# One sum in place of two: the attention values of a head group added up over all four key blocks at once, and a new order for every engine

## The chip, the core and the metric

The kernel runs on one core of a Trainium2 chip. The metric is the time of one execution in microseconds (us) of device time. The core has five engines that work side by side: TensorE (PE in the profile, with its weight loads as PEld), VectorE (DVE), ScalarE (ACT), GpSimd (POOL) and SyncE (SP), which starts the DMA transfers. Each takes its own instructions strictly in the order in which they stand in its queue, and waits with a semaphore where it needs another engine's result.

## The reference, cut to what matters

```
h   = x + attention(layernorm(x))           # x is 2048 x 512, 32 heads of 16
out = h + ffn(layernorm(h))                 # ffn: (gelu(g) * u) @ w_down, width 1376

attention, for each of 4 segments of 512 rows, one after the other:
    logits = (q @ k^T) / 4 + mask           # mask hides later keys
    a_dot  = softmax(logits) @ v
    a_mem  = (phi(q) @ M) / (phi(q) @ z + 1e-6)
    o      = g * a_mem + (1 - g) * a_dot    # g = sigmoid(beta), per head
    M, z  += phi(k)^T @ v, sum of phi(k)
then o @ wo
```

## The kernel before, in words

The program is written as a list of small operations (some 4,800), each bound to one engine. A table of numbers, `ORDER`, says in which order they are issued; from it follow each engine's queue and which buffer each operation gets, because a buffer is handed out at the first operation that uses it. [...]

The attention work is cut into 16 units, each a chunk of eight heads in one segment, and each unit into two head groups of four heads; there are 32 head groups, numbered Q0 to Q31 here. For one head group the steps are:

- `project` and `vproj` (L932, L981) make q, k and v on TensorE; DMA spreads q and k into tiles `stq` and `stk`.
- `pass_a` (L1186) computes the logits once to find each row's maximum. VectorE reads the maximum out of the PSUM bank (L1196, tiles `nm`), a small transpose (L1217) turns it, and a DMA writes it back into `stq`.
- `pass_b` computes the logits again, now transposed and with the maximum taken off: five `bank` blocks (L1244). Of the four key blocks of 128 keys, numbered 0 to 3, block 0 takes two of these, blocks 1 and 3 share two, and block 2 is the last. Each fills two PSUM banks; ScalarE takes the exponential into a `row` tile (L1250), GpSimd clears the part above the diagonal (L1258).
- `accum` (L1272) multiplies the exponentials with the values and adds up over the key blocks in one PSUM bank. It runs with four tiles of 32 columns each side by side. Before the change it is two operations: key blocks 0, 1 and 3 (12 matmuls) as soon as those four banks are done, and key block 2 (4 matmuls) after the last bank.
- ScalarE copies the sum out (L1291), and DMAs, VectorE and GpSimd normalise it. `mem` (L1134, L1154) adds the memory part, `mask`/`mup` (L1097) updates the memory.

TensorE is used in three modes: whole (128 rows by 128 columns: the feed forward network, L1531 and L1596), two halves of 64 rows (L932, L981, L1154, L1186, L1217, L1244, L1352), and four strips of 32 columns (L1097, L1134, L1272). All eight PSUM banks come out of one pool, and so do the 35 `row` tiles that hold the exponentials.

After the attention come the output projection (L1345, L1352), the second layer norm and the feed forward network in two halves of 1024 rows each. Some of it is interleaved with the last head groups.

Of the kernel before, what the change touches and what calls it, by code (L numbers as in the profile page):

```python
# [56 lines left out]
    76, 0, 5, 9, 6, 1, 10, 12, 4, 7, 13, 14, 8, 16, 27, 11, 91, 18, 92, 88, 93, 15, 17, 89, 19, 77, 28, 94, 29,  # L57
    167, 30, 25, 90, 21, 23, 20, 31, 102, 821, 33, 97, 46, 822, 47, 103, 104, 32, 95, 22, 34, 825, 44, 87, 35,
    36, 24, 168, 105, 37, 42, 106, 164, 107, 110, 826, 38, 108, 827, 40, 96, 26, 82, 111, 100, 43, 828, 84, 98,
    39, 41, 109, 118, 128, 45, 81, 824, 48, 51, 50, 829, 119, 165, 830, 831, 112, 130, 99, 113, 823, 129, 114,  # L60
    115, 1608, 116, 117, 133, 134, 78, 120, 140, 121, 122, 49, 138, 169, 166, 52, 832, 124, 53, 123, 139, 144,
    127, 833, 834, 2, 835, 54, 135, 85, 55, 75, 131, 3, 132, 145, 1026, 146, 136, 137, 147, 150, 149, 148, 170,
    56, 181, 58, 253, 172, 634, 1024, 186, 254, 255, 151, 171, 256, 59, 57, 176, 1028, 184, 185, 188, 126, 182,
    190, 125, 187, 101, 141, 142, 189, 152, 257, 154, 74, 162, 143, 183, 153, 177, 179, 60, 836, 258, 178, 173,
    61, 180, 1029, 175, 67, 68, 1025, 174, 837, 62, 63, 191, 625, 192, 259, 631, 65, 64, 69, 260, 79, 70, 66,
    193, 194, 195, 197, 71, 72, 198, 632, 261, 73, 213, 214, 262, 161, 270, 196, 263, 838, 272, 199, 273, 438,
    2986, 628, 158, 264, 268, 839, 439, 267, 239, 240, 241, 242, 440, 215, 243, 274, 269, 271, 229, 230, 232,
    276, 441, 840, 86, 275, 233, 442, 217, 216, 203, 224, 227, 225, 228, 226, 277, 266, 443, 231, 279, 234, 265,
    83, 237, 204, 235, 238, 205, 206, 236, 444, 1030, 841, 278, 200, 202, 445, 157, 1031, 207, 245, 842, 446,
    248, 449, 208, 246, 201, 843, 209, 450, 212, 448, 211, 633, 210, 244, 249, 247, 635, 218, 155, 250, 280,  # L70
    447, 1032, 219, 220, 221, 844, 222, 163, 845, 156, 846, 251, 847, 292, 848, 1033, 849, 295, 406, 286, 1034,
    407, 281, 296, 287, 852, 1035, 223, 282, 293, 297, 288, 408, 299, 318, 850, 300, 298, 301, 409, 410, 283,
    319, 80, 289, 321, 294, 328, 291, 329, 290, 302, 1027, 411, 304, 636, 303, 306, 313, 159, 331, 305, 307,
    412, 316, 314, 361, 362, 363, 364, 365, 323, 308, 324, 326, 626, 332, 317, 413, 320, 353, 354, 355, 366,
    367, 368, 369, 370, 414, 327, 797, 322, 818, 1036, 315, 427, 428, 1417, 309, 310, 330, 815, 311, 312, 798,
    415, 432, 325, 434, 627, 356, 357, 358, 359, 360, 433, 252, 417, 418, 799, 416, 334, 335, 421, 422, 800,
    419, 801, 337, 333, 338, 336, 284, 339, 429, 430, 431, 420, 629, 630, 387, 1037, 285, 340, 390, 391, 350,
    351, 352, 371, 372, 388, 802, 377, 160, 380, 378, 379, 803, 392, 435, 398, 393, 395, 425, 804, 401, 436,
    396, 373, 375, 341, 374, 376, 437, 805, 399, 809, 482, 483, 484, 485, 486, 426, 808, 586, 342, 424, 806,
    389, 477, 478, 479, 480, 481, 394, 423, 587, 1038, 807, 382, 383, 384, 343, 1411, 381, 402, 2122, 466, 467,  # L80
    468, 588, 514, 385, 386, 515, 516, 517, 589, 344, 819, 1039, 345, 346, 503, 506, 504, 469, 470, 471, 397,
    493, 590, 472, 473, 474, 475, 476, 603, 607, 400, 591, 494, 496, 498, 592, 508, 820, 499, 501, 495, 511,
    505, 593, 541, 542, 497, 487, 347, 509, 543, 594, 816, 488, 781, 500, 544, 545, 518, 536, 512, 540, 608,
    510, 2113, 538, 489, 490, 507, 491, 492, 595, 1040, 609, 403, 502, 457, 539, 537, 614, 615, 596, 513, 519,
    1224, 613, 610, 458, 611, 404, 1041, 533, 1225, 612, 597, 520, 598, 1042, 817, 578, 600, 581, 602, 601, 534,
    521, 405, 535, 599, 1226, 567, 530, 579, 570, 568, 1227, 562, 571, 606, 563, 565, 546, 531, 1228, 532, 547,
    616, 1229, 548, 572, 580, 564, 573, 618, 604, 575, 348, 550, 649, 549, 582, 551, 552, 651, 617, 1230, 557,
    650, 560, 558, 1043, 767, 662, 664, 768, 553, 665, 555, 663, 554, 1231, 1420, 666, 522, 646, 648, 1418, 605,
    1232, 576, 657, 647, 661, 574, 660, 769, 652, 556, 659, 1233, 770, 1235, 656, 459, 1234, 658, 771, 566,
    1236, 654, 673, 851, 1414, 1044, 561, 1045, 569, 653, 674, 559, 577, 676, 583, 584, 683, 655, 772, 460, 524,  # L90
    525, 688, 773, 684, 678, 675, 677, 774, 686, 1046, 689, 1047, 667, 691, 685, 668, 681, 669, 1048, 679, 1049,
    1050, 1051, 1052, 727, 671, 690, 728, 729, 731, 670, 349, 775, 730, 776, 692, 694, 777, 461, 680, 717, 672,
# [1606 lines left out]
```

## Time and profile before

| | us |
|---|---|
| median of 3 runs | 746.51 |
| lowest and highest | 746.02 and 747.25 |
| the profiled execution | 746.94 |
| its span, first to last instruction | 745.2 |
| TensorE busy in the span | 729.3 (98%) |
| VectorE, ScalarE, GpSimd busy | 568.5, 511.5, 474.5 |

The profiled execution's time is 1.7 us longer than its span, and 0.43 us above the median of the runs. The attention fills the span up to about 391 us, the feed forward network the rest. TensorE's matmuls are pipelined, so one begins before the one ahead of it has ended: the time that a group of matmuls takes is read from its start to the start of what stands behind it, not from its duration.

### The profile page before, as it was taken

How to read it: one execution, taken by the hardware profiler on the slowest of the kernel's cores; microseconds unless marked ns; L12 is line 12 of the kernel's file. 1: busy time of each engine (PE TensorE's matmuls, PEld its weight loads, DVE VectorE, ACT ScalarE, POOL GpSimd, SP SyncE). 2: the span in 40 equal slices, each digit the busy share in tenths (PEclk: the TensorE clock that was granted, in tenths of full speed). 3: DMA queues.
4: the chain of work that ended last, by engine and by line, in shares of the span. 5: the costliest groups of instructions: out<-in, count | busy, mean ns of one | idle time of the engine just before them, and what ended most of it. 6: DMA issues, size and time to landing. Idle time of an engine off the chain costs nothing.

```text
span 745.2 us, 18708 instructions
## 1 busy us (share of the span) xinstructions
PE 729.3 (98%) x6496; PEld 582.5 (78%) x6496; DVE 568.5 (76%) x1812; ACT 511.5 (69%) x1078; POOL 474.5 (64%) x750
## 2 busy tenths in 40 slices
PE   7999999999999999999999999999999999999998
PEld 6887867777877777876768788888887878888886
DVE  6897879988887898899987547775688756565466
ACT  6898888797767878878676557755586453553641
POOL 5455425564536546876884887868797578659930
PEclk9999999999999999999999999999999999999999
DMA  7756647656657757776756685554334260000003
GB/s 268 203 142 163 173 127 190 177 131 189 175 155 206 211 155 200 185 219 197 194 186 219 215 258 158 108 134 103 106 106 129 67 210 19 0 1 1 0 1 113
DMA packets 89658, 107.92 MB, mean 145 GB/s; under 512 B 31468, under 2 KB 41884, under 8 KB 89564
## 3 DMA queue, kind: packets, MB, share of 16 engines
q1 hardware_dynamic: 89260, 106.34, 50.2%
q8 instruction: 51, 0.84, 0.5%
q10 hardware_dynamic: 304, 0.39, 0.2%
q14 instruction: 43, 0.35, 0.2%
HBM read 57.03 MB, written 23.53 MB: 108 GB/s over the span
## 4 chain that ended last, share of the span: by engine, by line
PE 86%; DVE 8%; ACT 2%; issue 2%; DMA 1%; SPq 0%; DVEq 0%; ACTq 0%
PE bank L1531 28%; PE bank L1596 15%; PE bank L932 9%; PE bank L1272 8%; PE bank L1244 6%; PE bank L1186 5%; PE bank L981 5%; PE bank L1352 3%; PE bank L1345 3%; DVE bank L1196 2%; DVE aside L1196 2%; PE bank L1154 1%; DMA row<-wq 1%; DVE nm L1196 1%; PE bank L798 1%
## 5 line engine op out<-in xcount | busy, mean ns | idle before, releaser
L1250 ACT ACTIVATE row<-bank 128x512 f32<-128x512 f32 x309 | 165.5, 604 | 29.8 <-PE bank L1244 25.4
L1258 POOL TENSOR_SCALAR_AFFINE_SELECT row<-row 128x256 f32<-128x256 f32 (+1 forms) x309 | 105.9, 367 | 89.9 <-ACT row L1250 87.6
L1196 DVE CUSTOM_DVE_ANT_0 aside<-bank,amask 128x384 f32<-128x384 f32 (+2 forms) x384 | 141.7, 419 | 17.4 <-PE bank L1186 10.2
L932 PE MATMUL bank<-slot,slot 64*128 64x512 f32 x720 | 114.3, 403 | 0.0
L1531 PE MATMUL bank<-slot,slot 128*128 128x512 f32 (+1 forms) x399 | 106.1, 391 | 0.0
L1196 DVE CUSTOM_DVE_ANT_0 bank<-bank,amask 128x512 f32<-128x512 f32 x128 | 86.5, 710 | 12.0 <-PE bank L1186 10.1
L1531 PEld LDWEIGHTS bank<-slot,slot 128*128 128x128 f32 (+1 forms) x399 | 73.6, 186 | 17.5 <-issue 0.4
L1501 POOL TENSOR_TENSOR slot<-row,slot 128x512 fp32r<-128x512 f32 (+2 forms) x55 | 61.6, 1125 | 39.9 <-ACT slot L1499 37.6
L1186 PE MATMUL bank<-stk,stq 64*128 64x512 f32 (+3 forms) x512 | 82.0, 331 | 2.6 <-DMA stq<-slot 0.9
L1244 PE MATMUL bank<-stq,stk 64*128 64x384 f32 (+3 forms) x512 | 81.4, 333 | 1.7 <-DVE nm L1196 0.8
L1604 DVE TENSOR_TENSOR row<-row,bank 128x512 f32<-128x512 f32 (+1 forms) x91 | 60.4, 677 | 29.6 <-PE bank L1596 29.2
L1272 PE MATMUL bank<-row,vaug 128*32 128x512 f32 (+3 forms) x988 | 78.8, 436 | 1.2 <-DVE z L1145 0.4
L932 PEld LDWEIGHTS bank<-slot,slot 64*128 64x128 f32 x720 | 73.0, 185 | 6.2 <-DVE nm L1196 0.7
L1186 PEld LDWEIGHTS bank<-stk,stq 64*128 64x128 f32 x512 | 56.5, 185 | 14.4 <-DVE nm L1196 3.7
L1244 PEld LDWEIGHTS bank<-stq,stk 64*128 64x128 f32 x512 | 56.1, 185 | 14.6 <-DVE nm L1196 3.7
L1596 PE MATMUL bank<-slot,slot 128*128 128x512 f32 (+1 forms) x228 | 59.8, 389 | 0.0
L1272 PEld LDWEIGHTS bank<-row,vaug 128*32 128x32 f32 x988 | 30.5, 109 | 34.3 <-issue 27.3
L1531 PE MATMUL bank<-stk,slot 128*128 128x512 f32 (+1 forms) x198 | 54.7, 389 | 0.0
L981 PE MATMUL bank<-slot,slot 64*128 64x256 f32 x672 | 53.4, 284 | 0.0
L672 POOL TENSOR_TENSOR slot<-row,slot 128x512 fp32r<-128x512 f32 (+1 forms) x33 | 42.6, 1293 | 16.0 <-ACT slot L667 15.8
L1538 ACT ACTIVATE row<-bank 128x512 f32<-128x512 f32 (+1 forms) x54 | 31.6, 594 | 28.3 <-PE bank L1531 27.3
L1196 DVE DVE_READ_ACCUMULATOR2_ANT nm<- 128x1 f32 x512 | 50.1, 98 | 0.0
(269 smaller groups left out, 1622.4 us busy)
## 6 DMA issues: line engine op xcount, KB each, us to landing
stq<-slot SPq DMA_DIRECT2D x96, 128.0 KB
stk<-slot SPq DMA_DIRECT2D x94, 128.0 KB
row<-x SPq DMA_DIRECT2D x31, 256.0 KB
pv_dram<-row SPq DMA_DIRECT2D x31, 256.0 KB
row<-r_dram SPq DMA_DIRECT2D x27, 256.0 KB
row<-h_dram SPq DMA_DIRECT2D x23, 256.0 KB
row<-wd SPq DMA_DIRECT2D x17, 256.0 KB
row<-wu SPq DMA_DIRECT2D x16, 256.0 KB
```

The lines of the kernel that those rows point to most:

```text
L932: return nc.tensor.matmul(pm[i].t, w[i].t[rows_of(r), wi, dc * P:(dc + 1) * P], XT[s][dc].t[rows_of(r), xi, :], start=(dc, wi, xi, ph) == ...
L981: return nc.tensor.matmul(pms[n].t[:, 256 * t:256 * t + 256], XT[s][dc].t[rows_of(r), xi, t0:t0 + P], whl[wi].t[rows_of(r), dc // 2, 256 * ...
L1186: nc.tensor.matmul(sa.t[:, c0:c0 + w], sq.t[own, p, i * P:(i + 1) * P], sk.t[own, p, 0:w], start=True, stop=True, tile_position=(64 * a, 0 ...
L1196: nc.vector.tensor_tensor_reduce(out=(sa.t[:, c0:c0 + w] if i > 2 else aside[:, turns[0]:turns[0] + w]), in0=sa.t[:, c0:c0 + w], in1=amask ...
L1244: nc.tensor.matmul(sc.t[:, c0:c0 + D - q0], sk.t[own, p, q0:q0 + P], sq.t[own, p, q0:D], start=True, stop=True, tile_position=(64 * a, 0), ...
L1250: act(w, prio, lambda sc=sc, e=e: nc.scalar.activation(e.t[:, :w], sc.t[:, :w], AF.Exp), [sc, vtab], [e])
L1258: nc.gpsimd.affine_select(v, v, pattern=pat + [[1, P]], compare_op=OP.is_ge, fill=0.0, base=0, channel_multiplier=-1)
L1272: nc.tensor.matmul(pv.t[32 * n:32 * n + 32, kb * P:D], va.t[:, 136 * kb + 17 * j:136 * kb + 17 * j + 32], e.t[:, lo:lo + D - kb * P], star ...
L1501: pool(0.14 + 2.13e-3 * (hi - lo), prio, lambda: nc.gpsimd.tensor_tensor(v.t[:, 1, :hi - lo], r.t[:, lo:hi], v.t[:, 0, :hi - lo].bitcast(F ...
L1531: nc.tensor.matmul(dst.t[:w], v.t[:, wi, c0 + j * w:c0 + (j + 1) * w], b[bk][j].t[:, xi, :], start=first and j == 0 and n == 0, stop=j == ...
L1596: nc.tensor.matmul(pm.t[:, cs], HH[p, f, s].t[:w, hi, t * P:(t + 1) * P], v.t[:w, wi, cs], start=f == fl[0] and n == 0, stop=f == fl[-1] a ...
L1604: dve(W_, prio, lambda a=a, pm=pm, cs=cs, to=to: nc.vector.tensor_tensor(to.t[:, cs], a.t[:, cs], pm.t[:, cs], op=OP.add), [pm, a], [to])
```

## The change

The two `accum` operations of a head group become one, with all 16 matmuls, behind the last `bank` block; the key blocks are added in the order 0, 1, 3, 2. The matmuls themselves are the same. Lines of the new kernel lie 2 lower up to there and 3 lower behind (L1272 is L1270, L1531 is L1528).

The table `ORDER` has 32 entries fewer and is a new one from the first row to the last; only its start is shown. One argument `mode` is added to a VectorE operation of the feed forward network (f = 9), which the program reads for TensorE's operations alone.

```
@@ ORDER @@
-    76, 0, 5, 9, 6, 1, 10, 12, 4, 7, 13, 14, 8, 16, 27, 11, 91, 18, 92, 88, 93, 15, 17, 89, 19, 77, 28, 94, 29,
...
@@ -1281,9 +1279,8 @@
             bank([(p, 0, 0)])
         for p in range(2):
             bank([(p, 1, 0), (p, 3, 3 * P)])
-        accum((0, 1, 3), False)
         bank([(0, 2, 0), (1, 2, 2 * P)])
-        accum((2,), True)
+        accum((0, 1, 3, 2), True)
@@ -1561,7 +1558,7 @@
             lo(1.23 if f != 9 else D, prio, lambda: eng.tensor_tensor(
-                hh.t[:w, 1], e.t[:w], hh.t[:w, 0].bitcast(F32), op=OP.subtract), [e], [hh])
+                hh.t[:w, 1], e.t[:w], hh.t[:w, 0].bitcast(F32), op=OP.subtract), [e], [hh], mode=None if f != 9 else 'L')
```

Two places of the new order follow. The first is TensorE's queue around the sum of head group Q14, in the middle of the attention. L1244 are logits of the next head groups, L1186 is `pass_a`, L1097 the memory update, L1154 the memory part, L1272 the sum. A name such as `bank5_70` is a PSUM bank; the rows of the sum name the exponentials' tile and the values' tile. Before:

```order
L1272 MATMUL bank5_70<-row16_117,vaug1_141 32x128
L1272 MATMUL bank5_70<-row33_134,vaug1_141 32x128
L1244 MATMUL bank4_69<-stq0_96,stk0_91 128x512
L1244 MATMUL bank2_67<-stq0_96,stk0_91 128x512
L1186 MATMUL bank3_68<-stk2_93,stq2_98 128x512
L1186 MATMUL bank0_65<-stk2_93,stq2_98 128x512
L1097 MATMUL bank7_72<-vaug0_140,row11_112 32x34 x16
L1272 MATMUL bank5_70<-row31_132,vaug1_141 32x256
L1272 MATMUL bank5_70<-row3_104,vaug1_141 32x256
...
L1154 MATMUL bank2_67<-row9_110,mb5_151 128x256
L1154 MATMUL bank3_68<-row9_110,mb5_151 128x256
L1186 MATMUL bank4_69<-stk2_93,stq2_98 128x384
```

And now (lines 2 lower):

```order
L1270 MATMUL bank7_72<-row16_117,vaug1_141 32x256
L1270 MATMUL bank7_72<-row7_108,vaug1_141 32x256
L1270 MATMUL bank7_72<-row16_117,vaug1_141 32x256
L1242 MATMUL bank3_68<-stq0_96,stk0_91 128x512
L1242 MATMUL bank2_67<-stq0_96,stk0_91 128x512
L1184 MATMUL bank0_65<-stk2_93,stq2_98 128x512
L1184 MATMUL bank5_70<-stk2_93,stq2_98 128x512
L1215 MATMUL bank6_71<-ident_168,mm0_155 32x64
L1215 MATMUL bank7_72<-ident_168,mm0_155 32x64
L1152 MATMUL bank2_67<-row8_109,mb5_151 128x256
L1152 MATMUL bank0_65<-row8_109,mb5_151 128x256
L1184 MATMUL bank3_68<-stk2_93,stq2_98 128x384
```

Before, the sum's last part stood behind four matmuls of other work and the memory update; now it stands with the rest, ahead of them, and the memory update has moved to the next sum. Between `pass_a` into a bank (bank3 before, bank0 now) and the memory part into the same bank there stood the memory update and four matmuls of the sum; now there stand two small transposes.

The second place is the start of TensorE's queue. L894 transposes the four rows of tiles of the first segment, L953 is the first projection. Before:

```order
L894 MATMUL bank4_69<-ident_168,row0_101 128x128
L894 MATMUL bank5_70<-ident_168,row0_101 128x128
L953 MATMUL bank6_71<-slot0_73,slot5_78 128x256 x2
L953 MATMUL bank7_72<-slot0_73,slot4_77 128x256 x2
L953 MATMUL bank6_71<-slot0_73,slot5_78 128x256
L953 MATMUL bank7_72<-slot0_73,slot4_77 128x256
L953 MATMUL bank6_71<-slot1_74,slot5_78 128x256 x2
L953 MATMUL bank7_72<-slot1_74,slot4_77 128x256 x2
L894 MATMUL bank1_66<-ident_168,row2_103 128x128
```

And now:

```order
L892 MATMUL bank4_69<-ident_168,row1_102 128x128
L892 MATMUL bank5_70<-ident_168,row1_102 128x128
L892 MATMUL bank6_71<-ident_168,row3_104 128x128
L892 MATMUL bank7_72<-ident_168,row3_104 128x128
L892 MATMUL bank1_66<-ident_168,row3_104 128x128
L892 MATMUL bank0_65<-ident_168,row3_104 128x128
L892 MATMUL bank6_71<-ident_168,row2_103 128x128
...
L951 MATMUL bank3_68<-slot0_73,slot4_77 128x256 x2
```

Rows of the third and fourth tile were transposed in the middle of the projection before; now all four come ahead of it (of the last tile's four transposes three are left out).

## Rows read from the trace of the kernel before

**Rows 1.** The page: span, busy time of each engine, its 40 slices
```profile
span 745.2 us, 18708 instructions
PE 729.3 (98%) x6496; PEld 582.5 (78%) x6496; DVE 568.5 (76%) x1812; ACT 511.5 (69%) x1078; POOL 474.5 (64%) x750
...
PE   7999999999999999999999999999999999999998
...
PEclk9999999999999999999999999999999999999999
```

**Rows 2.** Three stretches (start, attention, feed forward): busy us and instruction counts
```profile
0.00:24.00 24.00, 18.16 (x131) 16.08 (x132) 15.65 (x51) 17.37 (x45) 15.19 (x36) 1.00 0.79 255
24.00:391.00 367.00, 361.11 (x4828) 280.58 (x4826) 321.68 (x1371) 296.61 (x656) 214.10 (x478) 1.00 0.65 178
391.00:742.00 351.00, 350.01 (x1542) 285.86 (x1542) 230.95 (x392) 197.51 (x378) 245.17 (x236) 1.00 0.35 102
```

**Rows 3.** The chain that ended last, shares by engine
```profile
PE 86%; DVE 8%; ACT 2%; issue 2%; DMA 1%; SPq 0%; DVEq 0%; ACTq 0%
```

**Rows 4.** What TensorE waited for: us in total, times, longest
```profile
PE bank L869 <- DMA row<-x: 3.9, 1, 3.9
PE bank L1186 <- DMA stq<-slot: 0.9, 1, 0.9
PE bank L1244 <- DVE nm L1196: 0.8, 2, 0.5
PE bank L1531 <- DVE row L1604: 0.6, 1, 0.6
```

**Rows 5.** TensorE in order of time around an undivided sum (start, us, count)
```profile
230.78 0.40 PE L1186 MATMUL bank<-stk,stq 64*128 64x384 f32 x4
231.02 0.91 PE L932 MATMUL bank<-slot,slot 64*128 64x512 f32 x6
...
232.00 0.40 PE L1244 MATMUL bank<-stq,stk 64*128 64x384 f32 x4
232.33 2.36 PE L1272 MATMUL bank<-row,vaug 128*32 128x512 f32 x32
234.62 0.96 PE L932 MATMUL bank<-slot,slot 64*128 64x512 f32 x6
```

**Rows 6.** The same around a divided sum, head group Q9
```profile
156.49 1.93 PE L1272 MATMUL bank<-row,vaug 128*32 128x512 f32 x24
158.35 0.23 PE L1217 MATMUL bank<-ident,mm 64*32 64x64 f32 x2
158.39 0.48 PE L1244 MATMUL bank<-stq,stk 64*128 64x384 f32 x4
158.81 0.64 PE L1272 MATMUL bank<-row,vaug 128*32 128x256 f32 x8
159.37 0.95 PE L1186 MATMUL bank<-stk,stq 64*128 64x512 f32 x2
```

**Rows 7.** The same around the sum of Q14, the place shown in the order
```profile
209.40 0.50 PE L1244 MATMUL bank<-stq,stk 64*128 64x512 f32 x2
209.74 0.40 PE L1186 MATMUL bank<-stk,stq 64*128 64x512 f32 x2
210.06 0.46 PE L1097 MATMUL bank<-vaug,row 128*32 128x34 f32 x32
210.34 0.66 PE L1272 MATMUL bank<-row,vaug 128*32 128x256 f32 x8
210.93 0.70 PE L1154 MATMUL bank<-row,mb 64*128 64x256 f32 x3
```

**Rows 8.** VectorE and ScalarE at that place (start, us, idle before)
```profile
210.17 0.70 DVE L1196 CUSTOM_DVE_ANT_0 bank<-bank,amask 128x512 f32<-128x512 f32 x1 [0.90 <-PE bank L1186]
...
210.05 1.09 ACT L1250 ACTIVATE row<-bank 128x512 f32<-128x512 f32 x2 [0.41 <-PE bank L1244]
```

**Rows 9.** GpSimd's clearing by form: busy, mean ns, idle before
```profile
L1258 POOL TENSOR_SCALAR_AFFINE_SELECT row<-row 128x256 f32<-128x256 f32 x185 | 73.7, 415 | 53.9 <-ACT row L1250 52.8 <-ACT mx L1221 0.4
```

**Rows 10.** Weight loads by line: busy, mean ns, idle before and its cause
```profile
L1186 PEld LDWEIGHTS bank<-stk,stq 64*128 64x128 f32 x512 | 56.5, 185 | 14.4 <-DVE nm L1196 3.7 <-issue 1.4 <-DVE slot L841 1.1
L1244 PEld LDWEIGHTS bank<-stq,stk 64*128 64x128 f32 x512 | 56.1, 185 | 14.6 <-DVE nm L1196 3.7 <-ACT row L1250 2.5 <-issue 1.6
...
L1272 PEld LDWEIGHTS bank<-row,vaug 128*32 128x32 f32 x988 | 30.5, 109 | 34.3 <-issue 27.3 <-POOL row L1258 1.6 <-POOL slot L672 0.8
```

**Rows 11.** The start, engines in order of time
```profile
8.88 0.98 DVE L675 TENSOR_TENSOR slot<-row,slot 128x512 fp32r<-128x512 f32 x1 [0.32 <-ACT slot L667]
...
9.17 0.39 PE L953 MATMUL bank<-slot,slot 128*128 128x256 f32 x1 [0.52 <-ACT ln L874]
...
11.10 1.04 PE L894 MATMUL bank<-ident,row 128*128 128x128 f32 x8
...
16.68 5.92 PE L994 MATMUL bank<-slot,slot 128*128 128x256 f32 x48
...
23.52 0.73 PE L1186 MATMUL bank<-stk,stq 64*128 64x512 f32 x6 [0.92 <-DMA stq<-slot]
```

More of the change, by code (lines that the diff above doesn't have):

```diff
@@ L1283, in pass_b @@
             bank([(p, 1, 0), (p, 3, 3 * P)])
-        accum((0, 1, 3), False)
         bank([(0, 2, 0), (1, 2, 2 * P)])
-        accum((2,), True)
+        accum((0, 1, 3, 2), True)
         pvs = Val(PPVS)
@@ L1563, in geglu @@
             lo(1.23 if f != 9 else D, prio, lambda: eng.tensor_tensor(
-                hh.t[:w, 1], e.t[:w], hh.t[:w, 0].bitcast(F32), op=OP.subtract), [e], [hh])
+                hh.t[:w, 1], e.t[:w], hh.t[:w, 0].bitcast(F32), op=OP.subtract), [e], [hh], mode=None if f != 9 else 'L')
             HH[p, f, s] = hh
```

518 rows, old and new, of the table ORDER are left out of this document.

## The prediction, made before the changed kernel was run

> **What bounds the kernel now.** I read the page's busy times first. TensorE is busy for 729.3 of 745.2 us, in every slice but the first and the last, at the full granted clock [rows 1]; no other engine comes near. The chain that ended last says the same: 86% of it is TensorE [rows 3]. Then the span in three stretches. In the feed forward part TensorE is busy for 350.0 of 351 us, so there is nothing to win there; in the attention it is busy for 361.1 of 367 us, 5.9 us short, with VectorE (321.7) and ScalarE (296.6) close behind it; the start has 5.8 us of idle time [rows 2]. The list of waits confirms that few are long: the first row of x, 3.9 us, then nothing above 0.9 [rows 4]. "Busy" hides small losses, though, because a matmul that is held up in the pipeline counts as busy. Those show in the starts of the rows and in the idle time of the weight loads: 14.4 and 14.6 us ahead of L1186 and L1244 [rows 10]. So a gain must come from one of three things: fewer matmuls (the change has none fewer), fewer changes of TensorE's mode, or fewer of these small waits.
>
> **The change part by part.** *The merge.* A sum's matmuls take the same time in one piece or two; what a piece costs beside them is the way in and out of the mode of four strips. Undivided, from the sum's start to the next start it is 234.62 - 232.33 = 2.29 us [rows 5]. Divided, 158.35 - 156.49 = 1.86 and 159.37 - 158.81 = 0.56, together 2.42 [rows 6]. One more exit costs 0.13 us. The way in: four matmuls of 64x384 and 64x128 ahead of the same mode take 231.02 - 230.78 = 0.24 us, ahead of the sum 232.33 - 232.00 = 0.33 [rows 5], so 0.09. A round trip is 0.22 us.
>
> How many go is counted from the whole order, not from the diff. Before, 24 of the 32 head groups already had both parts in one stretch of that mode, back to back or with only L1097 or L1134 (the same mode) between; 8 had other work between. Over TensorE's whole queue the stretches of this mode go from 39 to 34. Five round trips of 0.22 us are 1.1 us. TensorE is the bound, and nothing lies beside it that would hide this. Ends: 0.65 us (exits alone) and 1.8 us (all eight).
>
> The Trainium skill (TensorEngine Tiling (Array Packing), Key Properties) has a rule for this: changing the tiling mode drains TensorE, changing the tile within a mode does not. It gives no price and treats both directions alike; with the exit's 0.13 us both ways the sum would be 1.3 us. The rows show the way in as the cheaper one, and I keep them.
>
> *The later sum.* The merged sum starts behind the last logits, so its inputs must be ready by then. From logits to usable exponentials it takes, at Q14, from 209.40 (L1244) to 210.05 + 1.09 = 211.14 (two exponentials) [rows 7, 8] and one clearing of 0.42 [rows 9]: 2.2 us. In the new order key block 2 comes last in the sum, behind some 1.7 us of the sum's own matmuls, and its waits stand on its own four matmuls. With them, the least work on TensorE between a head group's last logits and the matmuls that read them is 2.9 us, where it was 2.8. For key block 0 fewer groups have under 2.5 us (2, before 4). So this costs nothing; the bound is the 1.6 us that L1272's loads now wait for L1258 [rows 10], lost once more or won. Exponentials are held a little longer and the sum's bank is taken later, which only moves buffers.
>
> *The new order.* It moves everything, and this is the uncertain term. For every block of matmuls that waits for another engine I took the last matmul on which that engine's work rests, and added up the TensorE work that the order puts between the two. Below 0.8 us there were 48 such places in the attention, now 66; between 0.8 and 3 us 463, now 441. What a tight place costs: the weight loads ahead of L1186 and L1244 idle 29.0 us over their 320 blocks [rows 10], 0.09 us each. A place that is not covered costs more. At Q14 the memory part L1154 took a bank of `pass_a`: L1186 starts at 209.74, VectorE reads the bank from 210.17 for 0.70 [rows 8], and L1154 starts at 210.93 [rows 7], 1.19 us after L1186, with L1097 and four matmuls of the sum in between. Now two small transposes are in between. `pass_a`'s matmuls take some 0.24 us (the row of four at 230.78) [rows 5], the transposes 0.1, an estimate, so about 0.85 us of the 1.19 is uncovered there. So 18 more tight places cost between nothing (covered by the engine being ahead) and 18 x 0.85; at 0.09 they cost 1.6 us. The 22 fewer places of the middle band give some of it back. I take 0.7 us, nearer to the weight loads' row, since that is a mean over all blocks.
>
> *Start and end.* At the start all four rows are transposed ahead of the first projection. The eight transposes took 1.04 us at most in the middle before; L953 began at 9.17, was held for the weight's low part (L675, to 9.86), and the second projection L994 began at 16.68 [rows 11]. Moved ahead, the transposes delay L953 by about that, but it then runs through; what matters is when q and k leave for their DMA, which `pass_a` awaits at 23.52 for 0.92 us. I take 0, between -0.9 (that wait gone) and +0.9 (as much again). In the feed forward part the one wait of 0.6 us [rows 4] may go or come back elsewhere: 0, between -0.6 and +0.6. The last outputs stand in the same pattern as before. The added argument on a VectorE operation changes nothing that is issued.
>
> *The sum.* 746.94 - 1.1 + 0.7 = 746.54 us against the profiled execution, which stands 0.43 above the median of the runs. Against the median: 746.1 us.
>
> **The rivals.** *Slower: tight banks.* If the 18 new tight places behave like the one at Q14 rather than like the mean block, TensorE stops at each. From 0.15 us each they outweigh the merge: 18 x 0.15 - 1.1 = +1.6. At 0.2 it is +2.5 and 749.0 us. For it: 0.85 us worked out at one place, and VectorE and ScalarE are 88% and 81% busy in the attention (321.7 and 296.6 of 367) [rows 2], so they are rarely ahead. Against it: the places under 0.8 us that were there before did not show as long waits [rows 4].
>
> *Faster: cover won.* The same count from the transposed maxima (L1217) to the logits that need them, a trip over ScalarE and a DMA, has a median of 5.1 us of TensorE work, before 4.3. If the new order takes away a third of the attention's 5.9 us of idle time [rows 2], 2.0 us, on top of the merge's 1.1, the time is 746.51 - 3.1 = 743.4 us. Against it: from the logits to the sum hardly anything is gained.
>
> *A wait inside the sum.* The Trainium skill (TensorE: Matmul & The Clock Gate, The mechanism) states that matmuls complete in queue order and none overtakes another. By that rule a late key block 2 would hold up all that stands behind, where the old order had other work to put in front. As a mechanism of this kernel: the 2.2 us from logits to cleared exponentials against 2.9 us of cover leave 0.7 us to spare at the tightest place; if GpSimd is that late in the eight groups that used to be divided, 8 x 0.2 = 1.6 us would eat the merge's gain: 747.0 us, inside the forecast's range. [...]
>
> *It does not do what it says:* the merge alone touches 8 of 32 groups, so most of what will be measured is the new order. That is in the counts above.
>
> **How the numbers follow.** About 0.2% (1.5 us) is what a measurement of this kernel can tell from no change: below 745.0 is faster, above 748.0 slower. The forecast, and the wait inside the sum with it, ends between them: 0.42. Cover won: 0.34. Tight banks: 0.24. The likeliest is no change that can be told, at 746.1 us, with its own range of 745.0 to 748.0. For 8 in 10 the range reaches into both others: from 743.0, a little past the case of cover won, to 749.4, past tight banks at 0.2 us each.
>
> **What would show it.** In the new profile the exits at 0.13 us should be five fewer, and every sum one row of 32 records of about 2.29 us to the next start; a longer one means a wait inside it. The idle time of the weight loads ahead of L1184 and L1242 (29.0 us together before) shows the tight places: 30 to 31 if I am right, 33 and more if tight banks win, 27 if cover does. At Q14 the memory part should start about 1.2 us after `pass_a`, with TensorE idle or held. The second projection should start near 16.7 us and `pass_a` near 23.5, and the feed forward part should keep its 350 us. I am wrong if the attention's end moves by more than 1.5 us either way, or if the difference lies in the start or in the feed forward part.

## The result, and the profile after

The new kernel takes 749.53 us (median of 17 runs, 748.91 to 750.15), the kernel before 746.51 us in runs on the same chip. The ratio is 1.0041, 95% interval 1.0033 to 1.0049: slower by 3.0 us, where no change (746.1 us) was forecast, and 0.13 us beyond the end of the range.

Line numbers of the new kernel are two lower than before (three lower behind the attention), of most experiments up to five. The page of the new kernel (its span, busy times, slices of TensorE and its granted clock) looks much as before [rows 1]:

```profile
span 747.7 us, 18747 instructions
PE 732.7 (98%) x6496; PEld 586.7 (78%) x6496; DVE 568.6 (76%) x1812; ACT 513.5 (69%) x1078; POOL 475.9 (64%) x750
...
PE   6999999999999999999999999999999999999998
...
PEclk9999999999999999999999999999999999999999
```

TensorE is "busy" 3.4 us longer with the same 6496 matmuls, so "busy" must count time in which matmuls are held. Neither it nor the three stretches, here as in [rows 2], tell where the loss is:

```profile
0.00:24.00 24.00, 17.18 (x126) 15.43 (x126) 16.47 (x50) 17.35 (x44) 17.53 (x40) 1.00 0.77 242
24.00:391.00 367.00, 362.29 (x4776) 283.41 (x4780) 319.44 (x1366) 293.30 (x653) 212.03 (x473) 1.00 0.65 177
391.00:742.00 351.00, 350.98 (x1591) 286.08 (x1583) 230.09 (x393) 202.84 (x383) 246.39 (x238) 1.00 0.35 101
```

What tells it is the starts of the matmuls. Both kernels issue the same blocks, a block being the matmuls of one operation. The start of a block, set against the TensorE work (the blocks' own durations) that lies ahead of it, shows which kernel is behind, and by how much. A block's *excess* is the distance from the start of the block ahead, less that block's duration and 0.1 us for a change of mode. Worked out from all blocks of the two profiled executions:

| TensorE work done | where | before, us | after, us | after behind by | changes of mode | excess so far, us |
|---|---|---|---|---|---|---|
| 16 us | first `pass_a` | 23.28 | 24.18 | 0.90 | 1, 1 | 3.3, 3.3 |
| 30 us | | 38.38 | 40.02 | 1.63 | 1, 1 | 4.4, 5.2 |
| 180 us | mid attention | 206.41 | 207.49 | 1.07 | 37, 31 | 18.8, 19.6 |
| 220 us | | 250.05 | 253.52 | 3.48 | 49, 41 | 21.3, 24.7 |
| 340 us | attention's end | 386.03 | 389.62 | 3.58 | 82, 72 | 33.9, 37.7 |
| 687 us | last blocks | 735.57 | 738.12 | 2.56 | 83, 73 | 36.4, 39.1 |

So: start +0.9; attention +2.7, made of 10 changes of mode fewer (-1.0, at the 0.1 us set for each) and 3.8 us more excess (34.4 against 30.6); feed forward part -1.0. Each profile is one execution. The kernel "old to 391" below has the same order up to there as the kernel before, and its profile is 1.7 us ahead of that one between the first `pass_a` and the attention's end: 0.9 of it is one place near 176 us. So the attention's terms are good to some 2 us.

The start in TensorE's rows, to set beside [rows 11]: four rows of x are transposed first, and the first projection waits for them, then runs through. The row shown first is that of the kernel before, where the first transposes start 0.52 us earlier.

```profile
7.19 1.47 PE L894 MATMUL bank<-ident,row 128*128 128x128 f32 x8
```

```profile
7.71 1.35 PE L892 MATMUL bank<-ident,row 128*128 128x128 f32 x8
9.32 1.09 PE L892 MATMUL bank<-ident,row 128*128 128x128 f32 x8 [0.26 <-DVE row L883]
11.43 6.02 PE L951 MATMUL bank<-slot,slot 128*128 128x256 f32 x48 [1.01 <-DVE slot L899]
17.28 5.92 PE L992 MATMUL bank<-slot,slot 128*128 128x256 f32 x48
24.42 0.50 PE L1184 MATMUL bank<-stk,stq 64*128 64x512 f32 x2 [1.22 <-DMA stq<-slot]
```

The wait of the feed forward part [rows 4, its last row] is gone, and the one for the first row of x is 4.8 us where it was 3.9. What TensorE waited for is now:

```profile
PE bank L867 <- DMA row<-x: 4.8, 1, 4.8
PE bank L1184 <- DMA stq<-slot: 1.2, 1, 1.2
PE bank L951 <- DVE slot L899: 1.0, 1, 1.0
PE bank L1270 <- DVE nm L1194: 0.5, 2, 0.3
```

The weight loads, the row on which the prediction meant to read tight places, idle no longer than in [rows 10]:

```profile
L1184 PEld LDWEIGHTS bank<-stk,stq 64*128 64x128 f32 x512 | 59.5, 185 | 14.0 <-DVE nm L1194 3.8 <-ACT row L1248 2.3 <-DMA stq<-slot 1.4
L1242 PEld LDWEIGHTS bank<-stq,stk 64*128 64x128 f32 x512 | 57.7, 185 | 14.6 <-DVE nm L1194 3.0 <-issue 2.1 <-DVE tock L549 1.2
L1270 PEld LDWEIGHTS bank<-row,vaug 128*32 128x32 f32 x994 | 31.9, 109 | 33.0 <-issue 28.6 <-DVE nm L1194 0.8 <-POOL row L1256 0.6
```

The merged sums are as forecast: 25 of 32 take 2.29 to 2.31 us to the next start, the others 2.15 to 2.41, so nothing waits inside them. The place at Q14 [rows 7, 8] is one of the new stops: the memory part L1152 starts 1.03 us after `pass_a` (L1184). It is held by ScalarE (the ACT rows), which first copies a sum out (L1288) and then takes two exponentials (L1248); the first of these ends at 212.26, and L1152 starts at 212.32.

```profile
211.29 0.40 PE L1184 MATMUL bank<-stk,stq 64*128 64x512 f32 x2
211.53 0.53 PE L1215 MATMUL bank<-ident,mm 64*32 64x64 f32 x2
212.32 0.70 PE L1152 MATMUL bank<-row,mb 64*128 64x256 f32 x3 [0.26 <-ACT row L1248]
212.81 0.44 PE L1184 MATMUL bank<-stk,stq 64*128 64x384 f32 x1
212.86 0.38 PE L1152 MATMUL bank<-row,mb 64*128 64x256 f32 x1
...
211.18 0.60 ACT L1288 ACTIVATE row<-bank 128x512 f32<-128x512 f32 x1 [0.52 <-POOL row L1256]
211.67 1.08 ACT L1248 ACTIVATE row<-bank 128x512 f32<-128x512 f32 x2
```

Most stops repeat: in the profile of another kernel below that shares the new order behind 34 us, 545 of 606 blocks from 60 us on have the same excess within 0.015 us. Behind 34 us the new order has 38 blocks with an excess over 0.25 us, 15.2 us together; the same blocks had 2.3 us before. The old order has 22 such blocks, 10.5 us; after, these have 1.1. Each order has its own stops, and the new one has more.

### The profile page after: what moved, and what is told of

It reads as the page before. It is cut to its first block, busy times and chain, and to the rows that moved or that the text cites. A ratio compares the mean times of both kernels' runs of the same rounds, so it can differ in the third digit from the quotient of the medians.

```text
span 747.7 us, 18747 instructions
## 1 busy us (share of the span) xinstructions
PE 732.7 (98%) x6496; PEld 586.7 (78%) x6496; DVE 568.6 (76%) x1812; ACT 513.5 (69%) x1078; POOL 475.9 (64%) x750
## 4 chain that ended last, share of the span: by engine, by line
PE 83%; DVE 6%; DMA 3%; POOL 3%; ACT 2%; issue 1%; SPq 1%; ACTq 0%; DVEq 0%; POOLq 0%
PE bank L1528 28%; PE bank L1593 16%; PE bank L930 10%; PE bank L1270 7%; PE bank L1184 5%; PE bank L979 5%; PE bank L1242 5%; PE bank L1342 3%; DVE aside L1194 2%; PE bank L1349 2%; DVE bank L1194 1%; ACT row L1248 1%; PE bank L1152 1%; POOL row L1256 1%; DMA row<-wk 1%
## 5 line engine op out<-in xcount | busy, mean ns | idle before, releaser
L1248 ACT ACTIVATE row<-bank 128x512 f32<-128x512 f32 x312 | 166.3, 606 | 27.4 <-PE bank L1242 25.5
L1256 POOL TENSOR_SCALAR_AFFINE_SELECT row<-row 128x128 f32<-128x128 f32 (+1 forms) x312 | 106.5, 364 | 93.3 <-ACT row L1248 87.2
L1528 PE MATMUL bank<-slot,slot 128*128 128x512 f32 (+1 forms) x348 | 93.2, 390 | 0.0
L1184 PE MATMUL bank<-stk,stq 64*128 64x384 f32 (+3 forms) x512 | 86.5, 333 | 1.5 <-DMA stq<-slot 1.2
L1242 PE MATMUL bank<-stq,stk 64*128 64x384 f32 (+3 forms) x512 | 85.3, 336 | 0.7 <-DVE z L1143 0.3
L930 PEld LDWEIGHTS bank<-slot,slot 64*128 64x128 f32 x720 | 76.9, 185 | 5.9 <-DVE nm L1194 0.6
L1601 DVE TENSOR_TENSOR row<-row,bank 128x512 f32<-128x512 f32 (+1 forms) x79 | 52.4, 677 | 37.5 <-PE bank L1593 37.0
L1270 PE MATMUL bank<-row,vaug 128*32 128x512 f32 (+3 forms) x994 | 75.6, 436 | 1.1 <-DVE nm L1194 0.5
L1528 PEld LDWEIGHTS bank<-slot,slot 128*128 128x128 f32 (+1 forms) x348 | 64.8, 187 | 14.8 <-DVE vaug L1601 0.4
L1184 PEld LDWEIGHTS bank<-stk,stq 64*128 64x128 f32 x512 | 59.5, 185 | 14.0 <-DVE nm L1194 3.8
L1498 POOL TENSOR_TENSOR slot<-row,slot 128x512 fp32r<-128x512 f32 (+2 forms) x48 | 55.3, 1158 | 19.6 <-ACT slot L1496 19.4
L1270 PEld LDWEIGHTS bank<-row,vaug 128*32 128x32 f32 x994 | 31.9, 109 | 33.0 <-issue 28.6
L1528 PE MATMUL bank<-slot,stq 128*128 128x512 f32 (+1 forms) x192 | 52.2, 389 | 0.0
L979 PEld LDWEIGHTS bank<-slot,slot 64*128 64x128 f32 x672 | 49.5, 186 | 1.8 <-DVE nm L1194 0.8
L1560 POOL TENSOR_TENSOR slot<-row,slot 128x512 fp32r<-128x512 f32 (+1 forms) x23 | 29.8, 1299 | 19.5 <-ACT slot L1557 19.5
```

The lines of the kernel that those rows point to most:

```text
L930: return nc.tensor.matmul(pm[i].t, w[i].t[rows_of(r), wi, dc * P:(dc + 1) * P], XT[s][dc].t[rows_of(r), xi, :], start=(dc, wi, xi, ph) == ...
L979: return nc.tensor.matmul(pms[n].t[:, 256 * t:256 * t + 256], XT[s][dc].t[rows_of(r), xi, t0:t0 + P], whl[wi].t[rows_of(r), dc // 2, 256 * ...
L1184: nc.tensor.matmul(sa.t[:, c0:c0 + w], sq.t[own, p, i * P:(i + 1) * P], sk.t[own, p, 0:w], start=True, stop=True, tile_position=(64 * a, 0 ...
L1242: nc.tensor.matmul(sc.t[:, c0:c0 + D - q0], sk.t[own, p, q0:q0 + P], sq.t[own, p, q0:D], start=True, stop=True, tile_position=(64 * a, 0), ...
L1248: act(w, prio, lambda sc=sc, e=e: nc.scalar.activation(e.t[:, :w], sc.t[:, :w], AF.Exp), [sc, vtab], [e])
L1256: nc.gpsimd.affine_select(v, v, pattern=pat + [[1, P]], compare_op=OP.is_ge, fill=0.0, base=0, channel_multiplier=-1)
```

## The experiments

Each time is given as a ratio to the kernel before on the same chip, with its 95% interval; 0.001 is 0.75 us. Two versions are compared by their ratios, and such a difference is good to 1 or 2 us. "Old" and "new" are the orders of the two kernels, and times such as 189 us are those of the profiles.

### Which piece of the new order loses

Five pieced orders. The first three have every sum in two parts, in the new order one right behind the other. The last two keep the merge and take only the start from the old order. The edit in words:

```diff
 ORDER = [
-    ...
+    old up to the last matmul before t, then what is left in the new order
```

**Old to 391 us, then new (sums in two parts).** 

> The kernel before, its start and attention in the old order with the sums in two parts; only the feed forward part follows the new order. Theory (the loss is made by work handed over too tightly in the new order's attention and by its later start; its feed forward part wins): the feed forward part loses the one stall of 0.8 us at 568 us and some 0.2 more, so 746.5 - 1.0 = 745.5 us, ratio 0.9987. Rival (the feed forward part ran faster only because it came later or met other DMA traffic): 746.5, ratio 1.000.

Measured 0.9991 (0.9981 to 1.0000). Its profile shows the feed forward part 1.0 us shorter, as in the new kernel.

**Old to 189 us, then new.** 

> Old order up to 189 us, new order from there. Theory (tight places of the new order, most of them between 189 and 290 us): nothing at the start, then the +2.6 us that the new order gained on the clock between 189 and 391 us (1.03 to 3.56 behind), less 1.0 in the feed forward part: 748.1 us, ratio 1.0021. Rival (the late start is what counts, and what comes behind it only carries it on): 745.5 us, ratio 0.9987.

Measured 1.0056 (1.0042 to 1.0070), more than expected. By its starts it is 1.5 us behind the kernel before at the end of the first projection, in the same order (TensorE ran slowly there, see the last section), 0.7 at 160 us of work and 4.6 at the attention's end: the second half loses 3.9 us. Two of its six runs took 748.6 and 748.9 us, near the theory, the others 750.6 to 751.3; whether the slow start is the difference isn't known.

**New to 190 us, old to 391, then new.** 

> New order up to 190 us, old order from there to the end of the attention, new order in the feed forward part. Theory (tight places of the second half): the start and the first half cost 1.0 us, the second half nothing, the feed forward part wins 1.0: 746.5 us, ratio 1.000. Rival (late start): the start's delay is carried on and grows, 748 to 749 us, ratio 1.002 to 1.003.

Measured 1.0013 (1.0005 to 1.0022): 1.6 us more than with the old first half, and near the theory. The delay of the start doesn't grow behind it here.

**Old to 23.4 us, then new.** 

> The new kernel, but up to 23.4 us in the old order (142 instructions: the DMA of the first row of x goes first again, the first projection starts behind the first two transposes). Theory (the start's delay of 0.6 to 0.9 us is carried to the end): 0.6 to 0.9 us faster than the new kernel: 748.8 us, ratio 1.003. Rival (waits further back swallow it): as the new kernel, 749.5, ratio 1.004.

Measured 1.0089 (1.0066 to 1.0111). `pass_a` started 0.6 us earlier than in the new kernel, and then, until 29.7 us, TensorE waited for an instruction of ScalarE that the seam had put late; from its list of waits:

```profile
PE bank L1079 <- ACT vaug L1007: 2.7, 1, 2.7
```

So this run says nothing of what the start is worth.

**Old to 34 us, then new.** 

> The new kernel with the old order up to 34 us, where the two orders meet with less rearranged at the seam than at 23 us. Theory (the start's delay is carried to the end): 0.6 to 1.0 us faster than the new kernel, 748.7 us, ratio 1.003. Rival (later waits swallow it, or the old start leaves the new order's projections short of loads, as it did with the seam at 23 us): 749.5 us or more, ratio 1.004 or more.

Measured 1.0018 (1.0004 to 1.0032), 1.7 us less than the new kernel. By its starts it is 1.1 us ahead of it at the first `pass_a`, 1.4 at 30 us of work and 1.7 at the end. With the first of these five (0.9991) the ratios split the loss of 3.0 us: 1.7 for the start, 2.0 for the attention behind it (0.9991 to 1.0018, the merge's gain included) and -0.7 for the feed forward part, each good to about 1 us.

### What the merge is worth

```diff
+        accum((0, 1, 3), False)
         bank([(0, 2, 0), (1, 2, 2 * P)])
-        accum((0, 1, 3, 2), True)
+        accum((2,), True)
```

**New order, eight sums divided where nothing else has to move.** 

> The new order with the sum in two parts again; in eight head groups (0, 6, 8, 10, 18, 21, 25, 26) the first part goes forward to where banks and rows allow it with nothing else moved, so that other matmuls stand between the parts. 16 more changes of mode. Theory (a round trip costs 0.22 us and that is what the merge is worth): 8 x 0.22 = 1.8 us slower than the new kernel, 751.3 us, ratio 1.0065. Rival (the earlier first part takes a bank and stands in the way of what waits, so dividing costs several times its changes of mode): 753 us or more, ratio 1.009 or more. Rival (merged sums cost waits): not slower than the new kernel.

Measured 1.0070 (1.0047 to 1.0093), 2.2 us above the new kernel, where 1.8 was expected. Merged sums that cost waits are refuted; the size fits what the merge was said to win, but the interval reaches from 0.4 us to the first rival's 1.009.

**New order, six sums divided, the first part as far ahead as its inputs allow.** 

> The new order with the sum in two parts again, and in six of the eight head groups that used to be divided (2, 6, 9, 18, 26, 27) the first part 1.2 to 3.1 us of TensorE work ahead of the second, with other matmuls between: 85 changes of mode instead of 73. Theory (a round trip costs 0.22 us, and holding the exponentials for the merged sum costs nothing in this order): 6 x 0.22 = 1.3 us slower than the new kernel, 750.8 us, ratio 1.006. Rival (the merge itself costs: exponentials and banks held longer make the waits): faster than the new kernel, 748 us or less, ratio 1.002 or less.

Measured 1.0234 (1.0214 to 1.0255). The first part takes a bank 1.2 to 3.1 us of work earlier, at least six other instructions had to step back for it, and the excess grows from 39 to 53 us; some of it is TensorE's lower clock (0.50 from 167 to 174 us). Beside the run above it shows that where the part stands decides, not that there are two.

**Old order, all sums merged.** 

> The merged sum in the old order: each sum stands where its second part stood, and the few instructions that find no free buffer there step back until they do. TensorE's mode changes 81 times (84 before, 73 in the new order). Exponentials are held longer, so banks and slots come free later: 25 places have less than 0.5 us of TensorE work between the last matmul that a block rests on and the block (6 before, 9 in the new order). Theory (tight places cost 0.23 us each): 19 x 0.23 = 4.4, less 3 changes of mode at 0.11: 750.6 us, ratio 1.0055. Rival (the merge itself costs nothing, wherever it stands; only the new order's start and traffic cost): 746.2 us, ratio 0.9995.

Measured 1.0270 (1.0250 to 1.0289), 20 us slower: neither theory. At least 56 instructions had to step back for want of free rows and banks, and the excess is 48 us in the attention, before 30; here too the clock fell (last section).

**Old order, three sums merged, new feed forward part.** 

> Old start and attention, but with the sums of head groups 9, 10 and 26 in one piece, where the old order allows that with nothing else moved, and the new order in the feed forward part. For groups 2, 6, 14, 18 and 27 the old order has no place at which the whole sum finds its buffers. Theory (a round trip is worth 0.22 us each): 3 x 0.22 = 0.7 us faster than the same kernel with divided sums (ratio 0.9991 to the kernel before), ratio 0.9982, 745.2 us if the kernel before runs at 746.5. Rival (key block 2 comes late for a sum at the earlier place, waits of 0.3 to 0.5 us each): 0.3 to 0.8 us slower than that, ratio 0.9995 to 1.0002.

Measured 0.9985 (0.9971 to 0.9999): as expected from 0.9991 and three round trips (0.9982), but the gain over the divided sums is within the intervals. The medians of this version and of the kernel before are the same (746.36 and 746.38 us), so no gain over the kernel before is shown either.

### Tight places

My theory was that a block stops where little TensorE work lies between it and the last matmul that it rests on. A search moved single instructions by some places so that fewer blocks stand that tight (the order alone changes; the edit in words):

```diff
 ORDER = [
-    ...
+    the same instructions, fewer blocks under 1 us
```

**Mended in the attention.** 

> The new kernel, its start (24 us) and feed forward part untouched; in the attention blocks of matmuls and the instructions they rest on are moved by some places, so that fewer blocks stand close behind the matmul that they rest on: below 0.5 us 3 places (9 in the new order), to 0.8 us 35 (57), to 1 us 64 (105). TensorE's mode changes 79 times (73). Theory (tight places make the loss; measured mean excess 0.23, 0.15 and 0.06 us a place in these three classes, 0.036 beyond): 6 x 0.23 + 22 x 0.15 + 41 x 0.06 = 7.1 less, 69 x 0.036 = 2.5 and 6 x 0.11 = 0.7 more: about 3.9 us faster than the new kernel's 749.5, 745.6 us, ratio 0.999. Rival (the other engines are behind as a whole, so a wait that is removed comes back at the next block): within 0.5 us of the new kernel, 749 us, ratio 1.0035.

Measured 1.0054 (1.0035 to 1.0073). The 25th sum starts at 321.8 us, in the new kernel at 324.2. By 320 us of work 1.8 us of gain since the first `pass_a` are left, then a last sum at the seam waits 1.8 us for GpSimd:

```profile
PE bank L1268 <- POOL row L1254: 1.8, 1, 1.8
```

**The same with a later seam.** 

> As the kernel with mended tight places, but the mended order runs on to 420 us, so that the last sums are not held at the seam (2.3 us at 392 us there). Theory (tight places): the attention ends 2.0 to 2.5 us earlier than in the new kernel and the feed forward part takes up to 1 us more: 748 us, ratio 1.002. Rival (waits only move): 749 to 750 us, ratio 1.004.

Measured 1.0029 (1.0014 to 1.0043), 0.9 us below the new kernel, within the intervals and between theory and rival. Its profile has 48 blocks with an excess over 0.25 us, more than the new kernel's 39 from 24 us on, though it has 102 tight places instead of 171; some of the 48 lie where the granted clock was 0.50 in that profile (24.9 to 28.3 and 356.0 to 359.4 us).

**Mended everywhere.** 

> The merged kernel with an order mended everywhere, start and feed forward part too: 5, 41 and 74 places below 0.5, 0.8 and 1 us, 76 changes of mode. Theory (tight places): 4 x 0.23 + 16 x 0.15 + 31 x 0.06 = 5.2 less, 51 x 0.036 = 1.8 and 3 x 0.11 = 0.3 more, so 3.1 us, and some tenths at the start: 746 us, ratio 0.999. Rival (waits only move): 749 us, ratio 1.0035.

Measured 1.0046 (1.0028 to 1.0064): no gain in time. Here too the attention was ahead for a while: the 25th sum starts at 321.7 us (new kernel 324.2), the 31st at 389.2 (390.0).

**With the old start.** 

> All 32 sums merged; the old order up to 34 us, the new order's feed forward part, and between them the new order with its tight places mended: 2, 35 and 70 places below 0.5, 0.8 and 1 us of TensorE work (9, 57, 104 in the new order), 80 changes of mode. Theory (start and tight places are the whole loss and add up): 1.7 us less by the start and 2.0 us by the places, as the mended attention showed it: 745.8 us, ratio 0.999. Rival (the merge itself holds back a part: exponentials held longer): no better than the old start alone, 748.4 us, ratio 1.002.

Measured 1.0064 (1.0046 to 1.0083): 3.4 us worse than the old start alone.

**In the old attention.** 

> The old start, the old attention with sums 9, 10 and 26 merged and with its tight places mended in the same way (2, 25 and 60 below 0.5, 0.8 and 1 us, before 6, 42 and 104; 86 changes of mode, before 80), and the new order's feed forward part. Theory (a mended place wins some 0.04 us, as the mended attention showed: 2.7 us over 69 places): 65 x 0.04 = 2.6 less, 0.6 more by the changes of mode: 2 us faster than without, ratio 0.996, 743.5 us. Rival (the old attention's places stand where the engines are ahead; mending them only moves waits): ratio 0.9985 or above.

Measured 1.0013 (0.9999 to 1.0027): 2.1 us worse than without. In its profile the start met late weights and then a lower clock (2.2 us, last section). By the middle of the attention it had made that up, and in the second half it lost 3 us. The theory falls: the count of tight places doesn't foretell the time.

### Which engine holds TensorE

```diff
-                    def g(a=a, sa=sa, p=p, i=i, c0=c0):
-                        w = (i + 1) * P
+                    def g(a=a, sa=sa, p=p, i=i, c0=c0 + i * P):
+                        w = P
```

**VectorE's maxima cut, old order.** 

> The kernel before with VectorE's maxima cut: each of the 512 reductions of a logit bank reads only the last 128 of its 128 to 512 columns (part of the maximum is left out); order, buffers and TensorE's work are untouched. VectorE's 227 us on that line become some 110. Theory (VectorE is what TensorE waits for in the attention): much of the 21 us that matmuls and weight loads wait for VectorE goes; as the old order has fewer of these waits, it wins less than the new one: 5 to 12 us faster, ratio 0.985 to 0.993. Rival (the waits are for other engines or for transfers): within 2 us, ratio 0.997 to 1.

Measured 0.9872 (0.9852 to 0.9892): 9.5 us faster.

**The same, new order.** 

> The new kernel with the same cut of VectorE's maxima. Theory (the new order's extra waits are for VectorE): with VectorE free they go, and of the 3.0 us between the two orders there remain the start (+1.7), the feed forward part (-1.0) and the changes of mode (-1.1): as the kernel before with the same cut, within 1 us. Rival (they are waits for ScalarE, GpSimd, banks or transfers, set by the order as such): the 3 us between the two stay.

Measured 0.9893 (0.9874 to 0.9911). What the profile shows stands with the next run, which is of the same kernel.

**Again, for the profile.** 

> The new kernel with the cut of VectorE's maxima, a second time. Theory (the new order's extra waits in the attention are for VectorE): from 34 us to the end of the attention it is no slower than the old order with the same cut, 1 us faster by its fewer changes of mode, and what remains lies in the start (+1.7). Rival (part of the waits is for other engines, or set by the order as such): 1 to 3 us slower than it between 34 and 391 us.

Measured 0.9906 (0.9887 to 0.9926). The attention's window in both profiles, old order first:

```profile
24.00:391.00 367.00, 363.52 (x4875) 290.42 (x4872) 241.58 (x1385) 302.27 (x671) 221.11 (x484) 1.00 0.67 184
```

```profile
24.00:391.00 367.00, 362.51 (x4859) 286.17 (x4860) 238.04 (x1381) 300.23 (x669) 218.83 (x480) 1.00 0.66 184
```

VectorE falls from 320 to 240 us of 367, and both orders run 9.5 to 11 us faster. Yet of the 3.0 us between the orders 1.6 and 2.5 stay by the two timings (each within some 2 us). By the starts the new one loses 2.8 us from the first `pass_a` to the attention's end, with VectorE whole 2.7; one late DMA of maxima is 1.65 of the 2.8, where the uncut kernel had 0.42. From 34 us on, the stretch of the expectation, it loses over 3 us, so the theory that it loses nothing there falls. VectorE costs both orders some 10 us; of the difference it can be a part, and isn't shown to be the cause. Of the 38 stops, 18 went (7.1 us) and 20 stayed (8.0 us), the one at Q14 to the digit:

```profile
204.54 0.40 PE L1184 MATMUL bank<-stk,stq 64*128 64x512 f32 x2
204.78 0.53 PE L1215 MATMUL bank<-ident,mm 64*32 64x64 f32 x2
205.57 0.70 PE L1152 MATMUL bank<-row,mb 64*128 64x256 f32 x4 [0.26 <-ACT row L1248]
```

**ScalarE's exponentials cut, new order.**

```diff
-                act(w, prio, lambda sc=sc, e=e: nc.scalar.activation(
+                act(w, prio, lambda sc=sc, e=e, w=P if Q > 4 else w: nc.scalar.activation(
```

> The new kernel with ScalarE's exponentials cut from the fifth head group on (from some 100 us): each writes only the first 128 of its 512 columns (part of the exponentials is left out); VectorE's maxima are whole again. Behind 100 us 19 blocks with 7.4 us of excess did not mind the cut of VectorE, and 14 with 5.6 us did. Theory (the new order's own waits are for ScalarE, which frees the banks of logits): at least 12 of the 19 start on time, 4.5 of their 7.4 us go, and the attention ends 6 to 12 us earlier. Rival (they are held by something else, TensorE's own sequence or rows that are held for the merged sums): most of the 7.4 us stay.

Measured 1.0024 (1.0014 to 1.0033), 1.3 us less than the new kernel, though ScalarE's 293 us in the attention became 215:

```profile
24.00:391.00 367.00, 361.17 (x4792) 281.66 (x4796) 319.83 (x1368) 215.13 (x654) 212.11 (x475) 1.00 0.65 178
```

Of the 19 stops behind 100 us that did not mind VectorE, 4 went; 5.9 of 7.4 us stayed. At Q14 the stop halved: L1152 starts 0.68 us after L1184.

```profile
210.30 0.40 PE L1184 MATMUL bank<-stk,stq 64*128 64x512 f32 x2
210.53 0.51 PE L1215 MATMUL bank<-ident,mm 64*32 64x64 f32 x2
210.98 1.04 PE L1152 MATMUL bank<-row,mb 64*128 64x256 f32 x3
...
210.73 0.70 DVE L1194 CUSTOM_DVE_ANT_0 bank<-bank,amask 128x512 f32<-128x512 f32 x1 [2.14 <-PE bank L1215]
```

ScalarE held the start of that block, and there VectorE stands right behind it: it reads a bank of `pass_a` from 210.73 to 211.43, and the second half of L1152's matmuls waits for that and starts at 211.54. So a stop that one cut leaves can have two holders, and cutting one engine at a time doesn't tell. ScalarE explains a few places, not the rest.

## Why the prediction was wrong

- *The merge, -1.1 us.* The count is right: ten changes of mode fewer in the trace (83 to 73). The price fits: eight divided sums cost 2.2 us, 0.27 a round trip where 0.22 was used, but that run's interval is wide.
- *The later sum, 0.* Right inside the sum (2.29 us each). But "only moves buffers" was too light. By a count of the buffers the old order has no place for the whole sum in five of the eight head groups, and merging all sums in it cost 20 us. So the whole merge needs a new order.
- *The new order, +0.7 us.* This step failed. From the first `pass_a` to the attention's end the excess grew by 3.8 us. The method was at fault, not the price alone: of five kernels with 30 to 43% fewer tight places one was 0.9 us faster than the kernel it was made from, within the intervals, and four were 0.4 to 3.4 us slower. Two were 2.4 us ahead of the new kernel at the 25th sum and lost most or all of it behind. Single places, not their count, decide: 38 blocks stop in the new order that ran through before, and 22 the other way. At Q14 the forecast of about 1.2 us came near (1.03), but by luck: the holder named was VectorE's read of `pass_a`'s bank, and the one that ended last was ScalarE.
- *The start, 0 +-0.9.* Failed in the value taken, and a part was overlooked. `pass_a` came 0.9 us later, the upper end. Of that 0.52 us stand already at the first transposes, since the first row of x comes later (TensorE's first matmul is at 4.3 to 4.8 us in the nine profiles with the new start, at 3.5 to 4.0 in the ten with the old one); at the second projection it is 0.60 (17.28, before 16.68), and the DMA of q and k is awaited 0.3 us longer. The old start up to 34 us wins 1.7 us.
- *The feed forward part, 0 +-0.6.* -1.0 us, beyond its bound: some 0.7 at the stall behind VectorE's row near 568 us, 0.4 earlier.
- *The sum of the measured terms:* +0.9 - 1.0 + 3.8 - 1.0 = 2.7 us, as the two profiled executions differ (749.6 and 746.94). The attention's end moved by 3.6 us, over the 1.5 that the prediction named as the sign of being wrong.
- *The rival "tight banks", 749.0 us,* came within 0.5 us by number and not by its mechanism. Its sign in the profile, 33 us and more of idle weight loads, did not come (28.6): a held matmul need not show there.
- *A wait inside the sum* is refuted by the sums' rows. (Its 747.0 us also leaves out the +0.7 of the new order; with it the rival was 747.7.)

What stays open is why the new order stops where it does: 15 stops were removed by neither engine's cut alone, and for most of them the trace shows no releaser. Both engines cut together, and GpSimd, were not tried. In the profiles the second half of the attention is where they cost most.

## What to carry to other kernels

A static order hangs together: merging all sums in the old one cost 20 us, and moving the first parts of six sums forward in the new one 14 us, while a new order with the same merge is 3 us off. So a change that needs a new order has to be judged with several orders, and its own part measured by undoing it inside one of them. To find a loss that busy times hide, set the starts of equal blocks against the work done, and join the orders piece by piece; read the seam before you believe the total, and compare two profiles of the same order before you believe a difference of 1 or 2 us.

## What the runs showed of the hardware that was not expected

In some profiles a stop was followed by a lower clock of TensorE and cost more than its length. In the old attention with mended places TensorE waited 1.30 and 0.62 us; ScalarE had waited 1.0 us for the DMA of a weight ahead of it:

```profile
9.54 0.39 PE L950 MATMUL bank<-slot,slot 128*128 128x256 f32 x1 [1.30 <-ACT ln L871]
10.54 2.29 PE L950 MATMUL bank<-slot,slot 128*128 128x256 f32 x9 [0.62 <-DVE slot L672]
12.63 1.48 PE L891 MATMUL bank<-ident,row 128*128 128x128 f32 x8
```

and the granted clock (third number from the right) fell to 0.50, which is 1.2 GHz, and was still there while TensorE was busy again:

```profile
9.50:11.00 1.50, 0.84 (x3) 0.64 (x4) 1.47 (x4) 0.87 (x4) 1.33 (x2) 0.71 1.06 407
11.00:12.00 1.00, 1.00 (x7) 1.00 (x7) 1.00 (x4) 0.88 (x2) 0.00 (x0) 0.50 1.04 397
...
13.00:14.00 1.00, 1.00 (x9) 1.00 (x8) 0.00 (x0) 0.25 (x2) 1.00 (x2) 0.73 1.06 387
14.00:16.00 2.00, 2.00 (x20) 2.00 (x19) 1.76 (x7) 2.00 (x6) 1.47 (x8) 1.00 0.98 363
```

In the same kernel without the mending the waits were 0.51 and 0.60 us, the clock stayed at 1.00, and the same eight transposes took 1.04 us instead of 1.48:

```profile
8.76 0.38 PE L950 MATMUL bank<-slot,slot 128*128 128x256 f32 x1 [0.51 <-ACT ln L871]
9.75 1.34 PE L950 MATMUL bank<-slot,slot 128*128 128x256 f32 x9 [0.60 <-DVE slot L672]
10.91 1.04 PE L891 MATMUL bank<-ident,row 128*128 128x128 f32 x8
```

0.81 us of waiting more ended as 2.2 us at the end of the first projection. That the longer wait is what lowered the clock is argued from these two profiles, not shown. The kernel "old to 189 us" has the same start, waited no longer than 0.35 us in these rows, yet its nine matmuls of L950 take the 2.29 us that they take above at 0.50. Its granted clock is on record from 13.45 us on only, that of the kernel before from 8.00:

```profile
10.06 2.29 PE L950 MATMUL bank<-slot,slot 128*128 128x256 f32 x9 [0.35 <-DVE slot L672]
12.15 1.67 PE L891 MATMUL bank<-ident,row 128*128 128x128 f32 x8
```

In the old order with all sums merged, where TensorE was busy 7.1 of 10 us from 265 to 275 us, the clock was 0.50 in the next 5 us and a sum took 4.50 us instead of 2.29:

```profile
265.00:270.00 5.00, 3.65 (x41) 1.37 (x37) 3.37 (x11) 1.71 (x5) 0.36 (x2) 1.00 0.58 136
270.00:275.00 5.00, 3.41 (x46) 1.77 (x45) 1.93 (x9) 4.78 (x10) 2.64 (x7) 0.98 0.15 50
275.00:280.00 5.00, 4.60 (x64) 2.10 (x64) 3.77 (x13) 1.20 (x2) 0.41 (x1) 0.50 0.83 180
```

```profile
275.97 4.50 PE L1268 MATMUL bank<-row,vaug 128*32 128x512 f32 x32
```

The Trainium skill (TensorE: Matmul & The Clock Gate, "What's actually happening") says that the clock is throttled by default and activity releases it; these rows agree. In the new kernel itself the clock stayed at 1.00 in every stretch shown, so its 3 us are not of this kind.

TensorE's matmuls also don't all start in the order of their queue. At Q14 the first matmul of the next `pass_a` block (L1184) starts at 212.81 us, and the last one of L1152, which stands ahead of it, at 212.86; both use the mode of two halves. So the description of the engines ahead, and the prediction's rule that no matmul overtakes another, don't hold to the last step for the starts in that mode.
